# Batch 2's plain heads are turned by the DMA crossbar as its dilated heads are, its values load behind the crossing, and batch 3's dilated pairs are scored in one visit and multiplied in one

## The chip, the cores and the metric

The kernel runs on one core of a Trainium2 chip. It is one launch; the time is that of the device, in microseconds, and the number that counts is the median over several executions. One execution was taken by the hardware profiler; its times stand in the profile.

The engines that matter here: TensorE (PE; its weight loads are shown as PEld), VectorE (DVE), ScalarE (ACT), GpSimd (POOL) and SyncE (SP). Each has a queue of its own and works it off in order; they wait for each other through semaphores. DMAs are issued here by POOL (loads, which also cast f32 to bf16) and by SP (output stores, and DMA transposes through the crossbar).

## The reference

```python
def _attn_ref(q, k, v):                    # (8, 8, 576, 64) each
    B, H, S, D = q.shape
    scores = 1.0 / np.sqrt(D) * np.matmul(q, k.transpose(0, 1, 3, 2))
    rel = np.arange(S)[:, None] - np.arange(S)[None, :]
    mask_plain = (rel >= 0) & (rel < 32)
    mask_dil = (rel >= 0) & (rel < 128) & (rel % 4 == 0)
    # heads 0..3 have mask_plain, heads 4..7 mask_dil
    ...
    return np.matmul(attn, v)              # softmax over the masked scores

x = attn_out.transpose(0, 2, 1, 3).reshape(4608, 512)
h = np.maximum(x @ w_in, 0.0)              # w_in 512 x 2048
return (h * h @ w_out)                     # w_out 2048 x 512
```

## The kernel before

**Attention.** Eight batches (0 to 7) of 576 tokens and eight heads. Heads go in pairs: e = 0, 1 are the plain heads (0 to 3), e = 2, 3 the dilated ones (4 to 7). A token is 4m + r; its residue r takes the place of the dilation, so that a dilated head is four plain bands of 144 tokens. Scores come out transposed (keys on the partitions), are put through an exponential on ACT (L709), multiplied with a 0/1 mask on DVE (L711), and then multiplied with the values and with ones (numerators `o` and denominators `d`). To normalise, ACT takes the logarithm of `d` ("L", L685 and L686) and the exponential of its negative ("X", L695), and DVE multiplies (L698, and L700 for the first 16 tokens of each residue, whose sums lie apart, in `rest`: the left-over columns of other banks) into `xT`, the input of the FFN, a ring of four batches.

**Four ways to get q and k transposed.** Batches 0 and 1 are turned by TensorE. From batch 3 on, all heads are turned by DMA transposes from `qb`/`kb` into `qx`/`kx` (`cross`, L254, four per batch: k and q of tokens 0 to 255, then of the rest), and small copies put the pieces where the scores read them: "R" (`arrange`, L344 and L347: the ends of the dilated heads, eight copies), "K" and "Q" (L338, L336: the plain heads). Batch 2 (`XB`) is mixed: its dilated heads are crossed (h0 = H // 2 in `cross`), its plain heads are turned by TensorE (`trans_both`, 64 transposes at L272, copied out at L278 on DVE and L280 on ACT).

**Visits.** `quadrants(scs, pvs)` is one visit of TensorE: it scores up to two head pairs (`scs`) and multiplies up to two (`pvs`), in four 64 x 64 quadrants of the array at once (`issue`, L368). A first pair is scored into two `pa` banks (`main_s`), a second into two `pf` banks if there are products in the visit, else into `po` and `pd` (`extra`). PSUM has four `pf` banks, two `pa`, one `po` and one `pd`; the FFN's accumulators and output tiles are `pf`.

**FFN.** x @ w_in (L951), relu on ACT (L964), square on DVE (L967), then times w_out (L998), copied out by ACT or DVE (L1004) and stored by SP. The first four tiles have 256 tokens (16 groups of matmuls each), the others 512 (32 groups). Groups count on from 0: tile 3 (tokens 768 to 1023) is groups 48 to 63, the tile of tokens 1024 to 1535 begins with group 64.

**The order is written by hand.** `PROGRAM` lists, separated by "|", what is recorded after each group (the first entry before all groups): `L2:x0` is the crossing of batch 2's first part, `1s1` a step of batch 1, and so on. `steps` holds (group, rank, batch, code) for the later batches: "V032/20,21" scores pair 2 and multiplies pairs 0 and 1 of the batch before; "E20" is an exponential with its mask; "L2", "X2" a normalisation; "R00", "K00", "Q00" copies. Every engine gets its instructions in the order in which they are recorded. Around the change it stood so:

| after group | batch 2 | batch 3 |
|---|---|---|
| 32, 37 | crossing, first and second part | |
| 36 | values of the dilated heads, then the loads of batch 3's q and k, then the other values | |
| 44 | | crossing |
| 46, 47 | R copies; 64 transposes of the plain heads | |
| 48 | scores of pairs 2 and 3 (one visit) | |
| 54, 55, 59 | at 55 scores of 0 and 1 with products of 2 and 3 | R copies |
| 61 | products of 0 and 1 ... | ... with scores of 2 |
| 71 | | products of 2 with scores of 3 |
| 81 | | products of 3 with scores of 0 and 1 |
| 88 | | products of 0 and 1 |

Of the kernel before, what the change touches and what calls it, by code (L numbers as in the profile page):

```python
# [12 lines left out]
RES = 4  # L13
# [50 lines left out]
def kernel(  # L64
# [9 lines left out]
    nc = tc.nc  # L74
# [18 lines left out]
    MT = (66, M - 64)  # L93
# [157 lines left out]
    def cross(b: int, nm: str, part: int):  # L251

        n, m0, h0 = MN[part], MS[part], H // 2 if b == XB else 0
        nc.sync.dma_start_transpose(  # L254
            (qx if nm == "q" else kx)[b % 2][:, h0:, :, m0 : m0 + n].rearrange("p h c m -> p (h c) m"),
            staged(b, nm)[0:n, part, h0:, :].rearrange("p h x -> p (h x)"),
        )
# [4 lines left out]

    def trans_both(e: int):

        pools = ((ps_a, "pa"), (ps_a, "pa")) if e else ((ps_o, "po"), (ps_d, "pd"))
        for nm, copy, (pool, name) in zip("kq", (nc.scalar.copy, nc.vector.tensor_copy), pools):
            x = pool.tile([P, 1024], bf16, name=name)[:, 0:S].rearrange("p (r m) -> p r m", r=RES)
            t = staged(XB, nm)
            for r in range(RES):
                for a, m0 in enumerate(MS):  # L270
                    for hl, rows in enumerate(sides):
                        nc.tensor.transpose(  # L272
                            x[rows, r, m0 : m0 + MT[a]],
                            t[0 : MT[a], a, 2 * e + hl, D * r : D * r + D],
                            ident[0 : MT[a], 0 : MT[a]],
                        )
            if nm == "q":
                copy(qT[:, e, :, :], x)  # L278
            else:
                copy(k_flat(e).rearrange("p (m r) -> p m r", r=RES), x.rearrange("p r m -> p m r"))  # L280
# [21 lines left out]
    def load_v_rows(b: int, which="d01"):  # L302


        if "d" in which:
            vds[b] = vd_pool.tile([P, NE // 2, 2, RES * D], bf16, name="vd")
            for hl, rows in enumerate(sides):
                for e in range(NE // 2):
                    nc.gpsimd.dma_start(  # L309
                        vds[b][rows, e, :, :],  # L310
                        v[b, H // 2 + 2 * e + hl, 0:512, :].rearrange("(m p r) d -> p m (r d)", p=64, r=RES),
                    )
                for i in (0, 8):
                    nc.gpsimd.dma_start(  # L314
                        v_rows[b % 2][rows, NE // 2 :, i, :],
                        v[b, H // 2 + hl : H : 2, 64 * i : 64 * i + 64, :].rearrange("h p d -> p h d"),
                    )
# [9 lines left out]
    def arrange(b: int, what: str, g: int, jj: int, e=None, copy=nc.vector.tensor_copy):  # L327
# [42 lines left out]
    def quadrants(scs, pvs):  # L370
# [14 lines left out]
        for n, (b, e) in enumerate(pvs):  # L385
# [74 lines left out]
        for n, (b, e) in enumerate(scs):  # L460
# [6 lines left out]
            for g, c in todo:  # L467
                items = scored[n][g, c]
                if b == XB and not dil:
                    for i in range(NB) if c == g ^ crossed(b, e) else ():  # L470
                        z, y = 96 if i < 8 else 64, 96 * (i // 2)
                        out = byr(ps[i % 2][sides[c], y : y + z])
                        rows = sides[g]
                        items.append(
                            ("s", out, k_flat(e)[rows, 64 * i : 64 * i + 64], qT[rows, e, :, 16 * i : 16 * i + z // RES], z)
                        )
                    continue
# [196 lines left out]
    def natural_step(b: int, code: str):  # L674
        what, e = code[0], int(code[1])
        if what in "QKR":
            arrange(b, what, e, int(code[2]), *(int(x) for x in code[3:4]), *[nc.scalar.copy][: len(code) - 4])
# [3 lines left out]
        elif what == "L":  # L681
            _, d, rest = op[b, e]
            rec = recs[b, e] = r_pool.tile([P, 576], f32, name="rec")
            if rest[0][0] is rest[0][1]:
                nc.scalar.activation(rec[:, 0:512], d[:, :], ACT.Ln)  # L685
                nc.scalar.activation(rec[:, 512:576], rest[1][0], ACT.Ln)  # L686
# [581 lines left out]
```

## Time and profile before

| | us |
|---|---|
| runs | 297.08, 298.9, 307.21 |
| median | 298.9 |
| the profiled execution | 296.37 |
| its span (first to last instruction) | 294.6 |
| SP queue busy with DMA transposes of batch 2 (from, to) | 51.8, 57.1 |
| loads of batch 3's q and k issued on POOL | 55.7 to 59.1 |
| visits at groups 48, 55, 61, 71, 81 begin | 68.0, 74.7, 81.2, 91.1, 100.5 |

The profile gives, for each engine, the busy time, and for each instruction its line, its operands by the program's names (`xx` holds `qx` and `kx`, `pt` the exponentials, `rec` the reciprocals, `osb` output tiles), its start and length in us from the start of the span, and the idle time before it with what ended it (after "<-"). An "x3" behind a row means three instructions shown as one. The chain of waits is followed back from the last instruction, at each step to what released it. A DMA is shown where it is issued; the time to its landing is in a row of its own.

### The profile page before, as it was taken

The page shows a single profiled execution, that of the slowest core. Times are in us where ns is not written, and L with a number is a line of the kernel's source. Part 1 is how long each engine was busy: PE and PEld are TensorE (multiplying, and loading weights), DVE is VectorE, ACT ScalarE, POOL GpSimd, SP SyncE. Part 2 cuts the span into 40 slices and gives each one's busy share as a digit, 9 for nine tenths or more (in the row PEclk, how much of TensorE's full clock was granted, in tenths as well). Part 3 has the DMA queues.
Part 4 walks back from the last instruction along what each step waited for, and adds up shares of the span by engine and source line. Part 5 has one row for each costly group of instructions (what it writes and reads, how often), then busy time and mean ns, then how long its engine had stood idle before and what let it go on. Part 6 is the DMA issues. An engine that isn't in the chain of part 4 may idle for free.

```text
span 294.6 us, 8141 instructions
## 1 busy us (share of the span) xinstructions
PE 289.2 (98%) x3351; PEld 166.8 (57%) x3351; DVE 155.2 (53%) x452; ACT 187.5 (64%) x381; POOL 123.3 (42%) x208
## 2 busy tenths in 40 slices
PE   8999999999999999999999999999999999999995
PEld 7689646859555554555455545554554455445443
DVE  1786225646779656686659465947454244004400
ACT  6788636868778663988577657766776466127511
POOL 8686266756639959078563597000000000000000
PEclk9999999999999999999999999999999999999999
DMA  7999999999999999999999699012101200121022
GB/s 118 195 183 213 204 221 197 170 188 155 211 216 194 128 190 125 173 144 140 160 196 97 93 166 154 2 36 76 36 2 37 73 36 2 36 71 36 2 71 71
DMA packets 82996, 35.48 MB, mean 120 GB/s; under 512 B 52384, under 2 KB 78208, under 8 KB 82960
## 3 DMA queue, kind: packets, MB, share of 16 engines
q0 software_dynamic: 49056, 18.49, 54.8%
q1 hardware_dynamic: 33760, 16.38, 27.2%
q8 instruction: 26, 0.43, 0.6%
q10 hardware_dynamic: 144, 0.10, 0.1%
q14 instruction: 10, 0.08, 0.1%
HBM read 37.50 MB, written 9.44 MB: 159 GB/s over the span
## 4 chain that ended last, share of the span: by engine, by line
PE 96%; DMA 1%; issue 0%; POOL 0%; ACT 0%; DVE 0%; ACTq 0%; POOLq 0%
PE pf L998 43%; PE pf L951 43%; PE po L368 2%; PE pa L368 2%; DMA kb<-in_k_dram 1%; PE pf L368 1%; PE pa L773 1%; PE pd L368 1%; PE pf L825 1%; PE po L743 1%; PE pa L555 0%; PE po L863 0%; PE pd L879 0%; POOL qb L173 0%; PE pf L555 0%
## 5 line engine op out<-in xcount | busy, mean ns | idle before, releaser
L951 PE MATMUL pf<-xT,w_in 128*128 128x512 bf16 (+1 forms) x704 | 128.1, 341 | 0.0
L998 PE MATMUL pf<-w_out_sb,h2T 128*128 128x512 bf16 (+2 forms) x592 | 127.9, 373 | 0.0
L951 PEld LDWEIGHTS <-w_in 128*128 128x128 bf16 x704 | 77.9, 113 | 46.6 <-issue 0.5
L964 ACT ACTIVATE h2T<-pf 128x512 bf16<-128x512 f32 x144 | 84.2, 600 | 29.9 <-PE pf L951 29.5
L967 DVE TENSOR_TENSOR h2T<-h2T 128x512 bf16<-128x512 bf16 x144 | 60.7, 425 | 62.5 <-ACT h2T L964 59.8
L998 PEld LDWEIGHTS <-h2T 128*128 128x128 bf16 x592 | 56.1, 98 | 63.8
L1004 ACT COPY osb<-pf 128x512 f32<-128x512 f32 (+1 forms) x34 | 19.5, 575 | 52.2 <-PE pf L998 52.1
L322 POOL DMA_DIRECT2D vbd<-in_v_dram x80 | 43.5, 555 | 19.0 <-DMA kb<-in_k_dram 8.2
L173 POOL DMA_DIRECT2D qb<-in_q_dram x19 | 13.6, 721 | 12.0 <-DMA xx<-qb 10.2
L695 ACT ACTIVATE rec<-rec 128x576 f32<-128x576 f32 x24 | 16.4, 683 | 0.7
L709 ACT ACTIVATE pt<-pa 128x384 bf16<-128x384 f32 (+1 forms) x28 | 12.7, 498 | 6.3 <-DVE xT L700 3.6
L173 POOL DMA_DIRECT2D kb<-in_k_dram x19 | 13.3, 699 | 6.3 <-DMA w_in<-in_moe_w_in_dram 2.5
L195 POOL DMA_DIRECT2D vbd<-in_v_dram x16 | 10.9, 687 | 10.2 <-DMA kb<-in_k_dram 5.0
L698 DVE TENSOR_TENSOR xT<-po,rec 128x512 bf16<-128x512 f32 x14 | 9.7, 691 | 7.5 <-ACT rec L695 6.9
L314 POOL DMA_DIRECT2D vbd<-in_v_dram x20 | 12.0, 614 | 3.5 <-PE pf L951 1.6
L309 POOL DMA_DIRECT2D vd<-in_v_dram x20 | 12.2, 625 | 1.9 <-PE pf L368 1.8
L711 DVE TENSOR_TENSOR pt<-pt,mask_n 128x448 bf16<-128x448 bf16 (+1 forms) x20 | 7.1, 373 | 9.4 <-ACT pt L709 9.3
L711 DVE TENSOR_TENSOR pt<-pt,mask_f 128x384 bf16<-128x384 bf16 x24 | 8.4, 355 | 6.7 <-ACT pt L709 6.5
L698 DVE TENSOR_TENSOR xT<-pf,rec 128x512 bf16<-128x512 f32 x10 | 6.9, 691 | 8.2 <-ACT rec L695 8.2
L336 DVE COPY qT<-xx 64x576 bf16<-64x576 bf16 (+1 forms) x30 | 10.8, 358 | 0.6
L368 PEld LDWEIGHTS <-vbd 64*64 64x64 bf16 x328 | 8.1, 107 | 4.2 <-issue 3.4
L368 PE MATMUL po<-pt,vbd 64*64 64x96 bf16 (+2 forms) x196 | 8.7, 202 | 0.0
(153 smaller groups left out, 281.4 us busy)
## 6 DMA issues: line engine op xcount, KB each, us to landing
qb<-in_q_dram POOLq DMA_DIRECT2D x7, 320.0 KB, 6.9
kb<-in_k_dram POOLq DMA_DIRECT2D x7, 320.0 KB, 8.2
vd<-in_v_dram POOLq DMA_DIRECT2D x34, 64.0 KB, 4.9
w_out_sb<-in_moe_w_out_dram POOLq DMA_DIRECT2D x4, 512.0 KB, 13.7
out_dram<-osb SPq DMA_DIRECT2D x16, 128.0 KB, 4.7
qb<-in_q_dram POOLq DMA_DIRECT2D x6, 256.0 KB, 6.8
kb<-in_k_dram POOLq DMA_DIRECT2D x6, 256.0 KB, 7.7
out_dram<-osb SPq DMA_DIRECT2D x9, 160.0 KB, 3.8
```

The source lines that it names most:

```text
L173: nc.gpsimd.dma_start(t[p0 : p0 + n, part, h0:h1, :], src[b, h0:h1, t0 : t0 + RES * n, :].rearrange("h (p r) d -> p h (r d)", r=RES),)
L322: nc.gpsimd.dma_start(v_rows[b % 2][p0 + 16 * r : p0 + 16 * r + 16, e, :, :], v[b, 2 * e + hl, :, :].rearrange("(i m r) d -> r m i d", r=R ...
L368: nc.tensor.matmul(out, lhs, rhs, start=begin, stop=True, skip_group_check=True)
L695: nc.scalar.activation(rec[:, :], rec[:, :], ACT.Exp, scale=-1.0)
L698: nc.vector.tensor_tensor(out=tok[:, :, 16:M], in0=byr(o[:, :]), in1=byr(rec[:, 0:512]), op=ALU.mult)
L709: nc.scalar.activation(pt, sp[b, e][g][:, 0:n], ACT.Exp, scale=SCALE)
L711: nc.vector.tensor_tensor(out=pt, in0=pt, in1=mask, op=ALU.mult)
L951: nc.tensor.matmul(to, w_in_sb[piece][:, kt, c0 : c0 + 509 : 4], rhs, start=(kt == kts[0] and x == 0), stop=(kt == kts[-1] and x == per - ...
L964: nc.scalar.activation(hv, acc[u][:, :].rearrange("p (x n) -> p x n", x=per), ACT.Relu)
L967: nc.vector.tensor_tensor(out=hv, in0=hv, in1=hv, op=ALU.mult)
L998: nc.tensor.matmul(cur[m][:, c0:c1], h2[:, f, P * m : P * m + P], w_out_sb[:, f, c0:c1], start=(f == 0), stop=(f == NF - 1),)
L1004: (nc.vector.tensor_copy if last and part == 1 or tk0 == 3 * NT // 2 else nc.scalar.copy)(osb[:, c0:c1], cur[m][:, c0:c1])
```

## The change

- `cross` takes all eight heads of batch 2; `trans_both`, its transposes and copies, and the zeroing of padding rows for it (code "y") are gone. The plain heads of batch 2 are put in place by Q copies on DVE (groups 43 and 44) and K copies on ACT (groups 44 to 47), and scored in the way of the later batches.
- Batch 2's crossing is recorded after groups 30 and 31 instead of 32 and 37, so that its first part stands ahead of an output tile's three stores on SP. Its R copies move from group 46 to 39, ahead of batch 1's last normalisations (recorded after group 40).
- Batch 2's last values are loaded (`vwr`) ahead of batch 3's q and k instead of behind them. Code "v" now writes its placeholder tile with a small memset, and is also used once before batch 2's values.
- Batch 3: the visit at group 61 has only batch 2's products; pairs 2 and 3 are scored together at 71, and multiplied together at 79, with the scores of 0 and 1. R moves from 54, 55 and 59 to 62 and 63. The dilated heads of pair 3 of batch 3 are crossed over (`crossed`), and the loads of its values follow.
- In a visit with two scores of which the first is plain, and two products, the left-over columns lie otherwise (`rest`): numerators in both `pa` banks, denominators in the first `pf` score bank and the second `pa` bank, for both pairs. Before, each pair had one bank for both: the second `pa`, the second `pf`. "L" reads the two halves with two instructions, "X" multiplies them with two.

```diff
@@ PROGRAM (what moves) @@
-... L1:q00123 y L1:q10123 ... | 1t1dq 1cq1a | 1t1dk 1ck1 L2:x0 |  | 1s1 | 1e10 | 1e11 L2:vwd
-L3:q00123 L3:q10123 L2:vwr L2:vwp | L2:x1 1f10 | ... | L3:x f |  |  | 2t0 2t1 |  |  | v L3:Vd ...
+... L1:q00123 L1:q10123 ... | L2:x0 | 1t1dq 1cq1a L2:x1 | 1t1dk 1ck1 |  | 1s1 | 1e10 | 1e11 v
+L2:vwd L2:vwr L3:q00123 L3:q10123 L2:vwp | 1f10 | ... | L3:x f |  |  |  |  |  | v L3:Vd ...
@@ crossed @@
-        return int(1 <= b <= XB and e in (1, 3) or b >= NATURAL and e == 1 or b >= PAIRED and e == 0)
+        return int(1 <= b <= NATURAL and e in (1, 3) or b > NATURAL and e == 1 or b >= PAIRED and e == 0)
@@ cross @@
-        n, m0, h0 = MN[part], MS[part], H // 2 if b == XB else 0
+        n, m0 = MN[part], MS[part]
         nc.sync.dma_start_transpose(
-            (qx if nm == "q" else kx)[b % 2][:, h0:, :, m0 : m0 + n].rearrange("p h c m -> p (h c) m"),
-            staged(b, nm)[0:n, part, h0:, :].rearrange("p h x -> p (h x)"),
+            (qx if nm == "q" else kx)[b % 2][:, :, :, m0 : m0 + n].rearrange("p h c m -> p (h c) m"),
+            staged(b, nm)[0:n, part, :, :].rearrange("p h x -> p (h x)"),
         )
-    def trans_both(e: int):
...
@@ arrange @@
+        elif what == "K" and b == XB:
+            copy(
+                k_both[rows, g::2, hs, :].rearrange("p i h (m c j) -> p j h c i m", c=2, j=2)[:, jj, :, :, :, :],
+                kx[b % 2][src, hs, :, :].rearrange("p h c (i m) -> p h c i m", m=16)[:, :, :, g::2, :],
+            )
@@ quadrants @@
                 to = main_s[crossed(b, e)]
                 if full and scs[0][1] < NE // 2:
-                    to = (extra if n else main_s)[1]
-                rest = [to[:, 448:512]] * 2, [to[:, 384:448]] * 2
+                    rest = [t[:, 448:512] for t in main_s], [extra[0][:, 448:512], main_s[1][:, 384:448]]
+                else:
+                    rest = [to[:, 448:512]] * 2, [to[:, 384:448]] * 2
...
-                if b == XB and not dil:
-                    for i in range(NB) if c == g ^ crossed(b, e) else ():
...
@@ natural_step @@
+            elif rest[0][0] is not rest[1][0]:
+                nc.scalar.activation(rec[:, 0:512], d[:, :], ACT.Ln)
+                for g in range(2):
+                    to = sides[g ^ crossed(b, e)]
+                    nc.scalar.activation(rec[to, 512:576], rest[1][g][to, :], ACT.Ln)
...
             for g, rows in enumerate(sides) if rest[0][0] is not rest[0][1] else [(0, slice(0, P))]:
+                if rest[0][0] is not rest[1][0]:
+                    g = g ^ crossed(b, e)
@@ run @@
-        if code == "y":
-            for nm in "qk":
-                nc.gpsimd.memset(staged(2, nm)[64:80, 0, 0 : H // 2, :], 0.0)
...
-            vd_pool.tile([P, NE // 2, 2, RES * D], bf16, name="vd")
+            nc.gpsimd.memset(vd_pool.tile([P, NE // 2, 2, RES * D], bf16, name="vd")[0:32, 0, 0, 0:2], 0.0)
@@ steps @@
     for x, code in enumerate(("R00", "R01", "R10", "R11")):
-        steps.append((46, 0, XB, code))
+        steps.append((39, 0, XB, code))
+    for x, code in enumerate(("Q00", "Q01", "Q10", "Q11")):
+        steps.append((43 + x // 2, 1, XB, code))
+    for x, code in enumerate(("K00", "K01", "K10", "K11")):
+        steps.append((44 + x, 1, XB, code + "a"))
...
             if early:
-                visit(start, [(b, 2)], [(XB, 0), (XB, 1)])
+                visit(start, [], [(XB, 0), (XB, 1)])
                 for y, e in enumerate((1, 0)):
                     steps.extend([(start + y, 3, XB, f"L{e}"), (start + y + 1, 0, XB, f"X{e}")])
-            expo(2, *((start + 3, start + 6) if early else (start + 7, start + 9)))
-            visit(second, [(b, x)], [(b, 2)])
-            norm(2, second)
-            expo(x, second + 3, second + 5)
+                visit(second, [(b, 2), (b, 3)], [])
+                expo(2, second + 1, second + 2)
+                expo(3, second + 4, second + 6)
+            else:
...
         if early:
-            visit(t + 17, [(b, 0), (b, 1)], [(b, 3)])
-            expo(0, t + 18, t + 18)
-            expo(1, t + 18, t + 18)
-            norm(3, t + 18)
+            visit(t + 15, [(b, 0), (b, 1)], [(b, 2), (b, 3)])
+            steps.extend((t + 15, 3, b, f"E1{x}") for x in range(2))
+            norm(3, t + 15)
+            expo(0, t + 16, t + 16)
+            norm(2, t + 17)
...
-            steps.append(((59, 59, 54, 55)[x] if early else at + x, 1, b, code))
+            steps.append((62 + x // 2 if early else at + x, 1, b, code))
```

More of the change, by code (lines that the diff above doesn't have):

```diff
@@ L261, in k_flat @@
         return kbd[:, e, :, :].rearrange("p i c -> p (i c)")[:, 0:S]
-    def trans_both(e: int):
[L265 to L280, printed above, removed]
     def blocks(b: int, e: int, part: int):
@@ L310, in load_v_rows @@
                         vds[b][rows, e, :, :],
[L311 removed]
+                        v[b, H // 2 + 2 * e + (hl ^ crossed(b, e + NE // 2)), 0:512, :].rearrange("(m p r) d -> p m (r d)", p=64, r=RES),
                     )
+                turn_ = hl * crossed(b, 3), (1 - 2 * hl) * crossed(b, 3)
                 for i in (0, 8):
@@ L468, in quadrants @@
                 items = scored[n][g, c]
-                if b == XB and not dil:
-                    for i in range(NB) if c == g ^ crossed(b, e) else ():
[L471 to L477, printed above, removed]
                 rows, h = sides[g], 2 * e + (c ^ crossed(b, e))
@@ L676, in natural_step @@
         if what in "QKR":
-            arrange(b, what, e, int(code[2]), *(int(x) for x in code[3:4]), *[nc.scalar.copy][: len(code) - 4])
+            es = {"e": int(code[3])} if code[3:4].isdigit() else {}
+            arrange(b, what, e, int(code[2]), **es, **({"copy": nc.scalar.copy} if code[-1] == "a" else {}))
         elif what == "V":
@@ L1125, in run @@
         elif code[0] != "L":
-            batch1(code[1:]) if code[0] == "1" else trans_both(int(code[2]))
+            batch1(code[1:])
         else:
```

10 lines of the change are left out of this document (6 added, 4 removed), and 20 rows, old and new, of the table PROGRAM.

## The prediction

> **What bounds the kernel now.** I read the page first: busy time, slices, chain; then the chain of waits in order of time; then, for the stretch that the change touches (47 to 102 us), the timelines of the SP queue, POOL, DVE and ACT.
>
> ```profile
> span 294.6 us, 8141 instructions
> ...
> PE 289.2 (98%) x3351; PEld 166.8 (57%) x3351; DVE 155.2 (53%) x452; ACT 187.5 (64%) x381; POOL 123.3 (42%) x208
> ...
> PEclk9999999999999999999999999999999999999999
> DMA  7999999999999999999999699012101200121022
> ...
> PE 96%; DMA 1%; issue 0%; POOL 0%; ACT 0%; DVE 0%; ACTq 0%; POOLq 0%
> ```
>
> TensorE is the bound: 289.2 of 294.6 us, 96% of the chain, its clock full in every slice. Two things follow. A matmul taken away is worth its time; and any wait put in front of TensorE is paid in full, because there is no idle time to absorb it (5.4 us in all). The DMA engines are full through the first half, where the change puts more on them.
>
> ```profile
> 65.71 0.40 PE po L272 x16
> 66.11 0.28 PE pd L272 x16
> 66.40 0.57 PE pa L272 x32
> 66.97 1.00 PE pf L951 x8
> 67.96 0.30 PE pa L368 x20
> ...
> 68.43 6.24 PE pf L951 x56
> ...
> 75.88 5.32 PE pf L998 x24
> ...
> 82.34 1.83 PE pf L998 x8
> 84.17 6.91 PE pf L951 x32
> ```
>
> In the chain of waits (start, us, what) the rows follow each other without a hole: TensorE goes from the transposes of batch 2 (L272) to the next FFN tile, to the dilated scores of batch 2 (L368), to the visit that ends at 75.88.
>
> **The change part by part.**
>
> (a) *Transposes gone.* All 64 of L272 leave the chain: 66.97 - 65.71 = **-1.26 us**. The instruction orders differ on TensorE by these 64 matmuls alone; the scores of batch 2 and the visits of batch 3 are only put in another order, 2 scores with 2 scores, 2 products with 2 products. From nothing to a few tenths: I take **-0.2**.
>
> (b) *Crossing all heads.* The four DMA transposes of batch 2 carry eight heads instead of four, and the small copies from them (R, eight on DVE) move from group 46 to group 39, ahead of the last four normalisations of batch 1.
>
> ```profile
> 51.78 1.28 SPq L254 DMA_TRANSPOSE xx<-kb  x1
> ...
> 55.94 1.20 SPq L254 DMA_TRANSPOSE xx<-qb  x1
> ...
> 65.66 1.49 SPq L254 DMA_TRANSPOSE xx<-kb  x1
> ...
> 72.97 3.23 SPq L254 DMA_TRANSPOSE xx<-qb  x1
> ```
> ```profile
> DMA to landing us min/median/max: 4.2/6.0/7.2
> ```
> ```profile
> DMA to landing us min/median/max: 6.3/7.7/8.4
> ```
> ```profile
> 49.28 0.67 POOL L195 DMA_DIRECT2D vbd<-in_v_dram  x1 [1.33 <-DMA kb<-in_k_dram]
> ```
>
> The first fence is the SP queue, the next two the time from issue to landing of batch 2's four transfers and of batch 3's four. Batch 2, four heads: first issue 51.78, last landing 55.94 + 7.2 = 63.1, so 11.4 us. Batch 3, eight heads: 65.66 to 72.97 + 7.7 to 8.4, so about 15.3. In the changed order the first pair stands ahead of three output stores, so it can go when k has landed: POOL's row, released by that landing, says 49.28. When is the last of the eight-head transfers down? Lower end, 11.4 us again: 60.7. Upper end, the work doubled: (11.4 - 4.2) x 2 + 4.2 = 18.6, so 67.9. The nearest row is batch 3's, the same size: 49.28 + 15.3 = 64.6; the three stores now stand between the two pairs. I take **65**.
>
> [...]
>
> ```profile
> 63.04 0.49 DVE L672 TENSOR_TENSOR xT<-pa,rec 128x320 bf16<-128x320 f32 x1 [0.34 <-ACT rec L668]
> 63.45 0.17 DVE L344 COPY kbd<-xx 64x128 bf16<-64x128 bf16 x1
> ...
> 64.81 0.30 DVE L347 COPY kbd<-xx 64x128 bf16<-64x128 bf16 x1
> ```
> ```profile
> 61.26 0.42 ACT L661 ACTIVATE rec<-pf 128x320 f32<-128x320 f32 x1
> ...
> 62.92 0.57 ACT L1004 COPY osb<-pf 128x512 f32<-128x512 f32 x1
> ```
> ```profile
> 50.17 0.70 ACT L560 COPY xx<-pa 128x640 bf16<-128x640 bf16 x1
> ```
>
> What is queued behind: R's first copy reads the last transfer, so DVE stands until 65. Behind it are eight copies (63.45 to 65.11: 1.66 us) and then the four L672. ACT's third L661 writes a buffer that the first L672 (0.49) has to free, so ACT stands too. From there, 61.26 to 62.92 (1.66 us) to the output copy L1004; after it the changed ACT order has three of the four new K copies (no such row; the nearest, 128x640 in 0.70, is twice as many partitions and from PSUM, DVE's 64-row copies are shorter: 0.6 each), then the second L1004. That frees the fourth `pf` bank for the next tile at landing + 1.66 + 0.49 + 1.66 + 0.57 + 1.8 + 0.57 = landing + 6.75. TensorE wants it after eight matmuls, the dilated scores and four more matmuls (0.111 each, 6.24 / 56): 68.43 + 0.45 = 68.9, less 1.26: 67.6. So the point from which it decides is a landing at 60.9, and every us after it costs one. At 65: **+4.1**; ends 0 and +7.0. In the kernel before, R came behind the L672, so a late landing held nobody. The other new copies (Q on DVE, the fourth K) replace those of L278 and L280 and lie beside FFN matmuls: nothing.
>
> (c) *Denominator ends in the score banks.* In a visit with two scores and two products the ends of rows now lie in both `pa` banks, and their denominators in the first `pf` score bank.
>
> ```profile
> 75.27 1.15 ACT L709 ACTIVATE pt<-pf 128x448 bf16<-128x448 f32 x2
> 76.31 0.59 ACT L685 ACTIVATE rec<-pf 128x512 f32<-128x512 f32 x1
> ...
> 77.64 0.91 ACT L709 ACTIVATE pt<-pa 128x448 bf16<-128x448 f32 x2
> ```
> ```profile
> 78.64 0.22 DVE L700 TENSOR_TENSOR xT<-pf,rec 128x64 bf16<-128x64 f32 x1
> ...
> 79.90 0.69 DVE L698 TENSOR_TENSOR xT<-po,rec 128x512 bf16<-128x512 f32 x1
> ```
> ```profile
> ACT pt L709 <- DVE xT L700: 3.6, 4, 0.9
> ```
>
> Before, the first exponential starts at 75.27, 0.6 us before the visit ends, and hands its bank to the matmul at 75.88. Now that bank takes denominators until the visit's last matmuls, so neither exponential starts before 75.9, and the next output tile gets the bank of the second: +1.15, the whole row. The same form occurs in the new visit of batch 3 at group 79: twice, **+2.3** (0.5 to 1.4 each).
>
> Then the exponentials at 77.64 read a bank that the L700 of the head before now reads too. That ACT waits for such a DVE read is in the waits (3.6 us in 4 cases); L700 ends at 78.86, so 1.2 later. Behind it on ACT are L685 and L695 of the next head, behind those the L698 that ended at 80.59, 0.6 before the next visit (81.20). With 0.6 + 1.2 more on ACT and 1.15 more on TensorE that leaves about nothing: **+0.3** (0 to 0.5).
>
> [...]
>
> (d) *Batch 3's R copies to groups 62 and 63*, ahead of an output copy on DVE.
>
> ```profile
> 82.11 0.60 ACT L685 ACTIVATE rec<-pf 128x512 f32<-128x512 f32 x1 [2.25 <-PE pf L368]
> ```
> ```profile
> 83.58 0.69 DVE L698 TENSOR_TENSOR xT<-pf,rec 128x512 bf16<-128x512 f32 x1 [1.51 <-ACT rec L695]
> ...
> 84.31 0.68 DVE L1004 COPY osb<-pf 128x512 f32<-128x512 f32 x1
> ```
>
> The copy frees the fourth bank of the next tile. It ends 2.9 us after the L685 that follows the visit; with four copies (0.83) ahead, 3.7, and 0.15 from the visit to L685: 3.9. TensorE wants the bank 1.83 (row 82.34) + 6 x 0.216 (6.91 / 32) = 3.1 after the visit: **+0.7** (0 to 1). The loads of batch 3's q and k are issued four small loads later on POOL; before, its first crossing waited for an output store on SP, not for them, so that costs nothing unless (b) is worse than taken. The two memsets that go and the two that come are on POOL, with nobody waiting.
>
> Sum: -1.26 - 0.2 + 4.1 + 2.3 + 0.3 + 0.7 = **+5.9 us**. The profiled execution took 296.4 us (span 294.6 and 1.8 around it), 2.5 below the median, 298.9; on the median that gives 304.8, and I say **305**. About 2% (6.0 us) is what a measurement of this kernel can tell from no change, so the forecast stands on the edge, just over it.
>
> **The rivals.**
>
> [...] Chance 0.2.
>
> *Only the gain*: the waits of (c) and (d) are hidden too, for instance if the bank handed to the next tile is an earlier one. -1.5, **297.4**. Against: TensorE's wait for the second exponential stands in the changed order. Chance 0.05.
>
> *The backlog goes on*: the transfers land at 67.9, so (b) is +7.0, batch 3's crossing, which waits on SP for the output copy that (b) holds up, lands later still, and its R copies stand on DVE at group 62 in front of the bank of (d). With the upper ends of (c) and (d): -1.3 + 7.0 + 2.8 + 0.5 + 1.0 = +10, **308.9**. It decides from a landing at about 67. [...] Chance 0.2.
>
> *Faster by over 2%*: 6 us would have to come out of 1.5 us of removed work and 5.4 of idle time. 0.03.
>
> **How the numbers follow.** The forecast has the rest, 0.52, and its own range of 302.5 to 307 (landing 63 to 67); three fifths of that lie over the bound, 304.9. Slower: 0.6 x 0.52 + 0.2 = 0.52. Faster 0.03. Within: 0.45. For 8 in 10 the range leaves out the gain and the far end of the backlog: 299.5 to 309.
>
> **What would show it.** (a) No L272. (b) A gap on DVE from about 59 us, ended by the DMA of the q crossing, longest among DVE's waits, ACT idle beside it, and a hole of TensorE at 66 to 70. If that copy starts before 61, (b) is wrong. (c) A hole of about 1.1 us after each visit at groups 55 and 79, ended by an exponential; without it, (c) is wrong. (d) A hole of some 0.7 after the first matmuls of the tile at group 64. A row of TensorE's clock under 9 in a slice would speak for the backlog.

## The result and the profile after

| | before | after |
|---|---|---|
| median of six executions, us | 297.7 (296.91 to 307.21) | 310.4 (309.67 to 312.24) |
| span of the profiled execution, us | 294.6 | 309.4 |
| mean granted clock of TensorE over that span (1 is full) | 1.000 | 0.983 |

The changed kernel is slower: ratio 1.044, 95% interval 1.041 to 1.048. The forecast was 305.0, from 299.5 to 309.0: the right side, 5.4 us short, and outside the range. (A ratio leaves out executions more than 1.5% above the fastest of the same kernel; where a kernel's executions spread widely it lies below the ratio of the medians.)

The page of the changed kernel, the rows that answer to those of before:

```profile
span 309.4 us, 8023 instructions
...
PE 294.5 (95%) x3287; PEld 168.3 (54%) x3287; DVE 159.1 (51%) x456; ACT 192.1 (62%) x383; POOL 121.2 (39%) x208
...
PEclk9999999996799999999999999999999999999999
...
PE 67%; DMA 24%; ACT 2%; DVE 2%; issue 2%; POOL 2%; SPq 0%; ACTq 0%; POOLq 0%
```

Two things are new. DMA has 24% of the chain of waits, which was almost TensorE's alone (96%); and TensorE is busy 5.3 us longer with 64 matmuls fewer, because its clock was under full in two slices, the tenth and eleventh (70 to 85 us). What TensorE waited for (us in total, times, longest):

```profile
PE pf L937 <- ACT osb L990: 3.2, 1, 3.2
PE pf L937 <- ACT rec L639: 2.3, 2, 2.1
PE pf L984 <- ACT pt L695: 2.0, 2, 1.0
PE po L729 <- DVE kbd L1008: 1.1, 1, 1.1
PE pa L354 <- DMA vbd<-in_v_dram: 0.8, 1, 0.8
PE pf L937 <- DVE osb L990: 0.7, 1, 0.7
PE po L354 <- DVE xT L682: 0.6, 1, 0.6
PE pf L937 <- DVE xT L882: 0.6, 1, 0.6
```

Only the fourth (L729, start-up) was there before; the last lies at 16 us, in the start as well. The first two belong to step (b), the third and the seventh to (c), the sixth to (d); the fifth, late values of batch 1, to none. (Lines of the changed kernel: L937 and L984 are the two FFN products, L990 the output copy, L354 the visits, L330 and L333 the R copies, L319 the K copies, L639 to L650 batch 1's normalisations, L695 the exponentials, L682 and L686 the multiplications of batches 2 and later, L253 the crossing.) The stretch in which most of the time went, in the chain of waits (start, us, what):

```profile
58.54 8.52 DMA xx<-qb
...
67.08 0.19 DVE kbd L330
...
69.07 0.53 DVE kbd L333
69.60 0.03 issue
69.63 0.50 DVE xT L650
...
71.83 0.57 ACT osb L990
72.40 1.52 ACT kbd L319
73.92 1.59 ACT kbd L319
75.53 1.31 ACT kbd L319
76.83 0.03 issue
76.86 0.59 ACT osb L990
77.45 0.04 issue
77.50 2.73 PE pf L937 x12
```

Here it can be read off in order what stood behind what: the last transfer of the crossing (down at 67.06), eight R copies until 69.60, a normalisation and the logarithms, an output copy, three K copies of 1.3 to 1.6 us, and the second output copy, whose bank TensorE had wanted for 3.2 us. The same stretch by windows (length, busy time and count of PE, PEld, DVE, ACT, POOL, granted clock, DMA share, GB/s):

```profile
66.00:70.00 4.00, 2.59 (x12) 1.09 (x11) 2.85 (x9) 0.00 (x0) 4.00 (x6) 1.00 1.37 153
70.00:74.00 4.00, 3.13 (x52) 2.17 (x52) 3.01 (x8) 3.77 (x7) 2.13 (x5) 0.71 1.61 184
74.00:78.00 4.00, 0.83 (x5) 0.44 (x4) 0.21 (x1) 3.94 (x4) 3.19 (x6) 0.50 1.75 183
78.00:82.00 4.00, 4.00 (x21) 2.74 (x20) 2.29 (x7) 3.94 (x9) 3.14 (x5) 0.51 1.41 192
82.00:94.00 12.00, 10.33 (x161) 7.06 (x159) 6.70 (x20) 7.88 (x17) 4.93 (x10) 1.00 1.44 181
```

The clock was full while TensorE stood at 68.6 to 70.6, half soon after, and full again from 82 on. A matmul at half clock looks like work, so the 3.7 us lost in this way show up nowhere among the waits.

Where the 14.8 us between the two profiled executions went, from the starts of the same pieces of work on TensorE's timeline:

| up to | later than before by, us | of which new | what |
|---|---|---|---|
| middle of batch 1's work (54.95, before 53.10) | 1.85 | 1.85 | the execution's start; the kernels are the same up to the loads; run 1, with the same start, was 0.2 ahead of before |
| output tile at 62.37 | 2.87 | 1.02 | late values of batch 1 (0.80 hole) |
| first tile after it, 70.64 | 3.74 | 0.87 | transposes gone -1.26, hole 2.06 |
| visit at group 55, 85.41 | 10.81 | 7.07 | holes 0.23 and 3.17, the rest (3.67) half clock |
| first matmul behind it, 87.74 | 11.88 | 1.07 | hole 1.02 |
| visit at 61, 93.73 | 12.60 | 0.72 | hole 0.65 |
| visit at 71, 104.70 | 13.69 | 1.09 | hole 0.72 in the tile of group 64 |
| products behind the visit at 79, counted behind the next visit, 123.36 | 14.94 | 1.25 | hole 1.02 |

Without the start it is 13.1, beside 12.7 between the medians.

### The profile page after: what moved, and what is told of

Same layout as the page of the kernel before. It is cut to its first block, busy times and chain, and to the rows that moved or that the text cites. A ratio compares the mean times of both kernels' runs of the same rounds, so it can differ in the third digit from the quotient of the medians.

```text
span 309.4 us, 8023 instructions
## 1 busy us (share of the span) xinstructions
PE 294.5 (95%) x3287; PEld 168.3 (54%) x3287; DVE 159.1 (51%) x456; ACT 192.1 (62%) x383; POOL 121.2 (39%) x208
## 4 chain that ended last, share of the span: by engine, by line
PE 67%; DMA 24%; ACT 2%; DVE 2%; issue 2%; POOL 2%; SPq 0%; ACTq 0%; POOLq 0%
PE pf L937 32%; PE pf L984 32%; DMA xx<-qb 7%; DMA qb<-in_q_dram 6%; DMA w_in<-in_moe_w_in_dram 3%; DMA w_out_sb<-in_moe_w_out_dram 3%; DMA vbd<-in_v_dram 2%; DMA kb<-in_k_dram 2%; ACT kbd L319 1%; PE po L354 1%; PE pf L354 1%; PE pa L354 1%; DVE kbd L333 1%; DMA out_dram<-osb 1%; POOL qb L172 1%
## 5 line engine op out<-in xcount | busy, mean ns | idle before, releaser
L937 PE MATMUL pf<-xT,w_in 128*128 128x512 bf16 (+1 forms) x704 | 131.5, 346 | 6.9 <-ACT osb L990 3.2
L984 PE MATMUL pf<-w_out_sb,h2T 128*128 128x512 bf16 (+2 forms) x592 | 127.8, 374 | 2.0 <-ACT pt L695 2.0
L937 PEld LDWEIGHTS <-w_in 128*128 128x128 bf16 x704 | 79.0, 115 | 56.1 <-issue 8.8
L953 DVE TENSOR_TENSOR h2T<-h2T 128x512 bf16<-128x512 bf16 x144 | 60.9, 425 | 63.2 <-ACT h2T L950 60.5
L984 PEld LDWEIGHTS <-h2T 128*128 128x128 bf16 x592 | 56.2, 98 | 65.8 <-issue 2.0
L990 ACT COPY osb<-pf 128x512 f32<-128x512 f32 (+1 forms) x34 | 19.5, 574 | 50.2 <-PE pf L984 50.0
L695 ACT ACTIVATE pt<-pa 128x384 bf16<-128x384 f32 (+1 forms) x26 | 11.7, 498 | 5.0 <-DVE xT L686 4.9
L194 POOL DMA_DIRECT2D vbd<-in_v_dram x16 | 10.9, 693 | 6.7 <-DMA kb<-in_k_dram 2.6
L682 DVE TENSOR_TENSOR xT<-po,rec 128x512 bf16<-128x512 f32 x13 | 9.0, 692 | 7.7 <-ACT rec L679 7.4
L682 DVE TENSOR_TENSOR xT<-pf,rec 128x512 bf16<-128x512 f32 x11 | 7.6, 692 | 10.3 <-ACT rec L679 10.3
L317 DVE COPY qT<-xx 64x576 bf16<-64x576 bf16 (+1 forms) x34 | 12.2, 360 | 0.6
L354 PEld LDWEIGHTS <-vbd 64*64 64x64 bf16 x328 | 8.8, 107 | 5.9 <-issue 4.4
L695 ACT ACTIVATE pt<-pf 128x448 bf16<-128x448 f32 (+1 forms) x18 | 8.3, 519 | 1.6 <-PE pf L354 1.0
```

What stands on the lines that cost most here:

```text
L354: nc.tensor.matmul(out, lhs, rhs, start=begin, stop=True, skip_group_check=True)
L682: nc.vector.tensor_tensor(out=tok[:, :, 16:M], in0=byr(o[:, :]), in1=byr(rec[:, 0:512]), op=ALU.mult)
L695: nc.scalar.activation(pt, sp[b, e][g][:, 0:n], ACT.Exp, scale=SCALE)
L937: nc.tensor.matmul(to, w_in_sb[piece][:, kt, c0 : c0 + 509 : 4], rhs, start=(kt == kts[0] and x == 0), stop=(kt == kts[-1] and x == per - ...
L953: nc.vector.tensor_tensor(out=hv, in0=hv, in1=hv, op=ALU.mult)
L984: nc.tensor.matmul(cur[m][:, c0:c1], h2[:, f, P * m : P * m + P], w_out_sb[:, f, c0:c1], start=(f == 0), stop=(f == NF - 1),)
```

## The experiments

Each kernel was run beside the kernel before; ratios are to that. Times are medians. Runs 1, 2, 3 and 5, and 8, have the changed kernel's line numbers; in the others the same lines are up to some 30 away.

**1. R behind the normalisations.** Theory 1 is that the order on DVE and the K copies on ACT make the holes, and the holes the half clock. Its rival is that the landing itself is what TensorE waits for.

```diff
-        steps.append((39, 0, XB, code))    # R00 R01 R10 R11
+        steps.append((40, 0, XB, code))
```

> Against the changed kernel only the order on DVE differs: batch 2's eight R copies stand behind batch 1's last four normalisations (group 40) instead of ahead of them (group 39). Theory 1 (the wait at the head of DVE's queue, then the slow K copies on ACT, make the holes at 68 to 78 us, and the holes bring the halved clock of 72 to 81 us): the 2.06 us hole ended by the logarithm L639 goes; the normalisations are over by about 66; the scores wait some 0.2 us for R (landing 67.06 + 2.55 = 69.6, TensorE there at about 69.5); the second output copy still stands behind three K copies of 1.5 us and ends at about 71.6, wanted at 70.6, so a hole of about 1 instead of 3.17. Holes 5.5 -> 1.3, and with no long hole the clock stays full, another 3.7: 310.4 - 7.9 = 302.5, range 300.5 to 305. Rival (it is the landing itself, TensorE needs what R writes in any order): the hole moves to the scores, the time stays within 1.5 us of 310.4.

Measured 301.58 us (four executions, 300.87 to 303.77), ratio 1.012 (1.006 to 1.018): 8.8 us less than the changed kernel, for one order of eight copies. DVE's timeline:

```profile
63.10 0.49 DVE L650 TENSOR_TENSOR xT<-pa,rec 128x320 bf16<-128x320 f32 x1 [0.34 <-ACT rec L646]
67.65 0.44 DVE L330 COPY kbd<-xx 64x128 bf16<-64x128 bf16 x1 [4.05 <-DMA xx<-qb]
67.76 0.48 DVE L333 COPY kbd<-xx 64x128 bf16<-64x128 bf16 x1
68.25 0.57 DVE L330 COPY kbd<-xx 64x128 bf16<-64x128 bf16 x1
68.36 0.61 DVE L333 COPY kbd<-xx 64x128 bf16<-64x128 bf16 x1
69.00 0.19 DVE L330 COPY kbd<-xx 64x128 bf16<-64x128 bf16 x1
```

DVE still stands 4 us for the same transfer, landed at 67.62, but with the normalisations behind it in time and not in the queue, nobody else stands with it. What TensorE now waits for lies at the scores of group 48, holes of 1.03, 0.97 and 0.65 us:

```profile
PE pa L354 <- DVE kbd L333: 1.6, 2, 1.0
PE pa L354 <- issue: 1.0, 1, 1.0
```

The first (1.03) has no releaser in the trace, but it ends at 67.71, just behind the landing, and the scores there read the transfer's own tile (`xx`); the other two wait for R. So the rival has a part of 1 us; for the rest theory 1 holds. The clock is not wholly saved: two of the four executions had a mean clock of 0.994 and took 302.2 and 303.8, the two with 1.000 took 300.9 and 301.0. The same program costs some 2 us more where the clock falls. How much of that is the clock and how much longer holes can't be told, since only one of the four has a trace.

**2. K copies on DVE.**

```diff
-        steps.append((44 + x, 1, XB, code + "a"))    # K00 K01 K10 K11
+        steps.append((44 + x, 1, XB, code))
```

> Against the changed kernel only this differs: batch 2's four K copies are made by DVE instead of ACT, after the same groups. Theory 1: the two output copies then follow each other on ACT, the second ends at about 73.0 instead of 77.45, before TensorE wants its bank (74.3): the hole of 3.17 us goes, the one of 2.06 before it stays. The clock still falls at 71.7, since that follows the first hole, but comes back earlier (it came back 4.4 us after TensorE went on): about 1.6 of the 3.7 us is saved. 310.4 - 3.2 - 1.6 = 305.6, range 303.5 to 307. Rival (the copies are as slow on DVE, 1.5 us each, and hold up the squares): no more than 1 us is gained. Rival (the second hole alone brings the clock down): the clock stays full, 303.5.

Measured 308.41 us, but from 304.17 to 311.94 in four executions; ratio 1.028 (1.017 to 1.038). The median is outside the expected 303.5 to 307. The 3.17 us hole is gone as theory 1 has it, and K on DVE took 0.88 each (3.51 for four), not 1.5. But the profiled execution, the slowest, had a new hole of 4.6 us at the tile of group 64, and DVE shows why:

```profile
91.57 0.21 DVE L686 TENSOR_TENSOR xT<-pa,rec 128x64 bf16<-128x64 f32 x1
95.73 0.19 DVE L330 COPY kbd<-xx 64x128 bf16<-64x128 bf16 x1 [3.94 <-DMA xx<-qb]
95.84 0.29 DVE L333 COPY kbd<-xx 64x128 bf16<-64x128 bf16 x1
96.14 0.19 DVE L330 COPY kbd<-xx 64x128 bf16<-64x128 bf16 x1
96.25 0.30 DVE L333 COPY kbd<-xx 64x128 bf16<-64x128 bf16 x1
96.39 0.68 DVE L990 COPY osb<-pf 128x512 f32<-128x512 f32 x1
```

Batch 3's last transfer landed at 95.7, and its R copies stand ahead of the output copy L990: the same trap as batch 2's, one batch later. That it shuts in some executions and not in others, by the landing of each, would explain the spread; only one has a trace. So this run alone could not price K; run 8 below does.

**3. Both.**

> Both edits: R behind the normalisations, K copies on DVE. Theory 1: nothing but the 0.2 to 0.3 us wait of the scores for R is left of the 5.5 us of holes, and the clock stays full: 310.4 - 5.2 - 3.7 = 301.5, range 300 to 303. What is left over the kernel before (297.7) is then the visits at groups 55, 61 and 79 and the tile at 64 (1.1 + 0.7 + 1.2 + 1.2), 1.0 for the late values of batch 1, less 1.26 for the transposes. Rival (the landing itself): within 1.5 us of 310.4.

Measured 301.60 us (300.69 to 305.69), ratio 1.012 (1.006 to 1.018), as expected, and no better than run 1: once R is out of the way, three K copies on ACT are over before TensorE wants the bank (in run 1 they lie at 64.90 to 69.46, and no wait for the second output copy is left). The profiled execution, the slowest at 305.69, again had the hole of the second trap (2.6 us, with half clock behind it).

**4. The second bank's exponential first** (at groups 55 and 79; the tile `pt` is now taken by whichever of the two comes first, which is not shown in the cut).

```diff
-    steps += [(55, 3, XB, "E10"), (55, 3, XB, "E11"), ...
+    steps += [(55, 3, XB, "E11"), (55, 3, XB, "E10"), ...
...
-            steps.extend((t + 15, 3, b, f"E1{x}") for x in range(2))
+            steps.extend((t + 15, 3, b, f"E1{x}") for x in (1, 0))
```

> Against the changed kernel only this differs: after the visits at groups 55 and 79 the exponential of the second score bank is made ahead of that of the first (ACT and DVE order alone). The second bank has no denominators of the rows' ends in it, so its exponential needn't wait for the visit's last matmuls, and the next output tile takes that bank. Theory (step c of the prediction: the hole of 1.02 us after each of the two visits is the wait for two exponentials in a row): each hole shrinks by 0.5 to 1.0, 310.4 - 1.5 = 308.9, range 308.2 to 309.5. Rival (the next output tile would then wait for the other bank, or something else is late): no change, 310.1 to 310.7.

Measured 309.77 us (308.76 to 310.70), 0.6 less than the changed kernel, inside the spread; the time doesn't decide. The trace does: the wait of L984 for L695 (2.0 us, twice 1.0) is gone from TensorE's list, and the second bank's exponential starts before the visit is over:

```profile
85.48 0.48 ACT L696 ACTIVATE pt<-pf 128x384 bf16<-128x384 f32 x1
86.24 0.54 ACT L696 ACTIVATE pt<-pf 128x448 bf16<-128x448 f32 x1 [0.27 <-PE pf L354]
```

Only the first bank's, with the denominators in it, still waits for the visit's matmuls (L354; L696 are the exponentials here). Ahead of the visit at 61 the hole grows from 0.65 to 1.3: TensorE is there earlier, ACT isn't.

**5. Run 1 and batch 3's R later** (groups 64 and 65 for 62 and 63).

> R of batch 2 behind batch 1's normalisations, as in the first run, and batch 3's R copies two groups later (64 and 65 instead of 62 and 63), behind the output copy of the tile before. Theory (step d of the prediction: R stands ahead of that copy on DVE, and where batch 3's crossing lands late the copy stands for it too): the hole of 0.66 us at the tile of group 64 goes, and so do the long ones (2.6 and 4.6 us with a halved clock behind them) that single executions of the two kernels with K on DVE had: 301.58 - 0.7 = 300.9, range 300.2 to 301.4, and a narrow spread. Rival (R's results are wanted just as early): the scores at group 71 wait instead, 301.5 or more.

Measured 301.36 us (300.17 to 302.86), ratio 1.013 (1.005 to 1.021). The 0.7 us hole at group 64 is gone from the trace, but the median is only 0.2 below run 1: too little to tell.

**6. R in the order of the landings, and both exponentials swapped.**

```diff
-    for x, code in enumerate(("R00", "R01", "R10", "R11")):
+    for x, code in enumerate(("R10", "R11", "R00", "R01")):
         steps.append((40, 0, XB, code))
```

> The kernel with both R moves, and two more orders changed: of batch 2's R copies the four that read the first tokens' transfers (landed at about 59.5) come first, so that only four, 1.1 us, are left after the last landing (67.6) instead of eight, 2.2; and the second score bank's exponential goes first at groups 55 and 79. Theory: the scores of group 48 start 1.1 us earlier, the holes of 2.65 us there shrink to about 1.5 and the clock, which fell for 3.3 us, stays full: -1.1 - 1.7; the two holes behind the visits go (-2.0) and 0.65 of it comes back ahead of the visit at 61, whose exponentials wait as before: -1.35. 300.9 - 4.1 = 296.8, range 296 to 299, so no slower than the kernel before (297.9). Rival (the clock falls again, since about 1.5 us of holes remain): 298.5. Rival (the landing, not the copies behind it, sets the scores): 299.5.

Measured 299.09 us (ten executions, 298.54 to 300.75), ratio 1.0067 (1.0035 to 1.0099). The clock stays full in the profiled execution (one of the ten has a mean of 0.993), four copies are made at 63 to 64, four after the landing, and of the 2.65 us of holes at the scores 1.4 are left. It is just outside the expected 296 to 299 and near the second rival's 299.5: the gain is smaller than forecast, because the transfer itself (67.1) now sets the scores.

**7. The crossing's second pair ahead of the stores, K on DVE.**

```diff
-... | L2:x0 | 1t1dq 1cq1a L2:x1 | 1t1dk 1ck1 | ...
+... | L2:x0 L2:x1 | 1t1dq 1cq1a | 1t1dk 1ck1 | ...
```

> As the run before, with batch 2's K copies on DVE, and with the crossing's second pair recorded right behind its first, ahead of the output tile's three stores on SP. Theory (the stores cost the second pair some 1.5 us in the queue): the last landing moves from 67.6 to about 66, the scores of group 48 wait for nothing, 296.8 - 1.0 = 295.8, range 295 to 297. Rival (the three stores now go some 5 us later, there are three output buffers, so the output copies at about 63 wait for them and the FFN's next banks with them): slower than the run before by 1 to 3 us. Rival (the transfers are limited by what the DMA engines carry): the landing stays at 67, no change.

Measured 299.06 us (ten executions, 297.16 to 303.58), ratio 1.0046 (1.0005 to 1.0086). The last landing is at 65.7 in place of 67.1, and TensorE's list has nothing of batch 2's crossing any more (the first row is the visit at 61; L720 and L928 are start-up, L975 four short gaps):

```profile
PE po L344 <- DVE xT L672: 1.3, 1, 1.3
PE po L720 <- DVE kbd L999: 1.1, 1, 1.1
PE pf L975 <- issue: 0.6, 4, 0.2
PE pf L928 <- DVE xT L873: 0.5, 1, 0.5
```

So in this order a landing by 66 is early enough; the prediction's 60.9 was for the order with R, the normalisations and the K copies behind the landing. In this trace TensorE waits for nothing that the late stores hold. The expected 295.8 was still missed by 3 us, and the executions spread over 6. The profiled one, 298.76, was 1.5 us late before batch 1's scores were over (54.58, before 53.10); what the slower ones lose, no trace shows. The run has two edits, and what each gave is not separated.

**8. K on DVE, batch 3's R later.** It prices K without the second trap.

> The kernel with K on DVE alone (R of batch 2 still ahead of the normalisations; 304 to 312 in single executions), and batch 3's R copies two groups later. Theory 1: the spread came from batch 3's crossing landing late (95.7) with its R copies ahead of an output copy on DVE; with R behind it, the second hole and its fall of the clock (4.6 + some 2.5 us in the profiled execution) can't happen, and what is left over the kernel with both moves is the hole at the head of DVE's queue (2 to 4 us at 66 to 70) and the half clock behind it (some 2.5 us): 304.5, range 303 to 306, narrow. The K copies then account for some 5 us of the changed kernel's time, the order of R for the rest. Rival (K on DVE was of no use, the 308 is what it is worth): 307 to 309.

Measured 304.48 us (304.13 to 305.62), ratio 1.024 (1.020 to 1.028): as expected, and narrow. That the spread is gone with batch 3's R behind the copy fits the second trap of run 2. What is left over run 1 is the hole at the head of DVE's queue (3.2 us in this trace, ended by L639) and the half clock behind it. With that, the changed kernel's K copies on ACT account for 5.9 us of its 310.4 (with the 0.7 of batch 3's R in it), the order of R for 8.8; the two overlap, since either edit alone keeps the second output copy from its long wait.

**9. Batch 3's part alone, on the kernel before.**

> The kernel before with only the batch 3 part of the change: pairs 2 and 3 scored together at 71 and multiplied together at 79 with the new places for the rows' ends, R at 62 and 63; batch 2 as before, its plain heads transposed by TensorE, its dilated heads alone crossed. Theory (steps c and d add up by themselves): one hole of 1.0 us after the visit at 79 and 0.7 to 1.2 at the tile of group 64, 297.9 + 1.9 = 299.8, range 299 to 300.6. Rival (these waits come only with the late crossing of batch 2): within 0.5 us of 297.9.

Measured 298.80 us (ten executions, 297.68 to 300.10), ratio 1.0043 (1.0011 to 1.0076), 1.6 over the kernel before in the same runs (297.17), where 1.9 was expected. Its waits are those of steps (c) and (d), each once (L721 are the exponentials there, L1016 the output copy, L963 and L1010 the FFN):

```profile
PE pf L1010 <- ACT pt L721: 1.0, 1, 1.0
PE pf L963 <- DVE osb L1016: 0.7, 1, 0.7
```

They add to 1.7. These costs don't come from the late crossing.

**10. All four exponentials of batch 2's plain heads ahead of the normalisations**, on top of run 7.

```diff
-    ... (55, 3, XB, "E10"), (55, 3, XB, "L3"), (56, 0, XB, "X3")]
-    steps += [(56, 1, XB, "E00"), (56, 1, XB, "E01"), (57, 3, XB, "L2"), ...
+    ... (55, 3, XB, "E10"), (55, 3, XB, "E00"), (55, 3, XB, "E01")]
+    steps += [(55, 3, XB, "L3"), (56, 0, XB, "X3"), (57, 3, XB, "L2"), ...
```

> As the kernel with the second pair ahead of the stores (299.06), and at group 55 all four exponentials of batch 2's plain heads stand ahead of the two normalisations. Theory: what is left there is the 1.3 us hole ahead of the visit at 61, which waits for the po bank that the second normalisation frees; ACT loses 1.14 us of that chain waiting for DVE's reading of the pa bank (L676) before the third exponential, and with the new order it doesn't: the hole shrinks to 0.2 to 0.5. 299.06 - 0.9 = 298.2, range 297.3 to 298.7; the medians of single executions with a late crossing stay. Rival (the first normalisation, now 0.9 us later on ACT, gives back a bank that the output tiles want): no gain, 299 or more.

Measured 297.23 us (twelve executions, 296.69 to 298.52), ratio 0.9996 (0.9973 to 1.0019): the change with these orders put right, and K on DVE, can't be told from the kernel before. The hole ahead of the visit at 61 is 0.4, as expected; the gain on run 7's median, 1.8, is twice the expected one, but the intervals of the two ratios overlap. In its profiled execution batch 3's crossing (down at 88.9) makes DVE late, and the products at 79 wait 1.3 us for masks: about what the missing transposes had saved.

**11. Batch 3's loads ahead of batch 2's last values**, on top of run 10.

> As the kernel with all four exponentials ahead (297.23, no different from the kernel before), and the loads of batch 3's q and k stand ahead of batch 2's last values on POOL again, as in the kernel before. Theory (the four loads that the change put in front make batch 3's crossing later: its last landing at 88.9 holds DVE for 4 us, and the products at 79 wait 1.3 us for DVE's masks): the landing comes 1 to 3 us earlier, the 1.3 us go: 296.2, range 295.5 to 297.0. Rival (batch 2's values then come late for the visits at 55 and 61): 298 or more. Rival (the DMA engines are full, the order of the loads changes only which of them lands first): the same as 297.2.

A miss of the expected 295.5 to 297.0: 298.85 us (twelve executions, 296.46 to 301.18), ratio 1.0027 (0.9993 to 1.0062). Batch 3's last landing came earlier, 83.2 in place of 88.9, but batch 2's came later, 68.0 in place of 64.0, and the scores of group 48 waited 1.9 us. Nothing waits for batch 2's values at the visits at 55 and 61, so the first rival has the time but not the cause. The second fits the landings, though it expected the time to stay at 297.2: in this stretch the order of the loads would only decide which transfer lands first. It isn't shown: there is one profiled execution of each, and runs 7 and 10, with the same order up to there, already differ by 1.7 us in batch 2's landing (65.7 and 64.0).

## Why the prediction was right in sign and short in size

**What failed is step (b): the landing and the K copies were too short in its sum, and the half clock that its hole sets off was not in it.** It put the freeing of the fourth `pf` bank at "landing + 6.75". The trace has 77.45 - 67.06 = 10.4. The terms:

| term | forecast, us | measured, us |
|---|---|---|
| last landing | 65 | 67.06 |
| TensorE's late start in this execution | none | -1.85 |
| R copies | 1.66 | 2.55 |
| normalisation to first output copy | 2.72 | 2.80 |
| three K copies on ACT | 1.8 | 4.4 |
| second output copy | 0.57 | 0.59 |
| half clock behind the bank | none | 2.2 |

The K copies were priced at 0.6 from two rows that were both unlike them: an ACT copy from PSUM and DVE copies of another layout. They were 1.5. Up to the visit at 55 the table of where the time went has 1.02 + 0.87 + 7.07 us, and with the 1.26 that the missing transposes gave back 10.2 us of losses, against +4.1. Of the difference, 3.6 are the longer way to the bank (0.9 of R, 2.6 of K), 0.2 the landing as TensorE saw it, and 2.2 the half clock of the 52 matmuls behind it (7.98 us on the timeline in place of 5.8 at 0.111).

**The landing looks right only by luck.** The first pair was issued at 48.09, 1.2 us ahead of the 49.28 that the step took, and the four transfers took 19.0 us instead of 15.7; that the 2.1 us cost so little is due to an execution in which TensorE was itself 1.85 late. In runs 1 to 6 and 8 the landing is at 66.9 to 67.6, with TensorE on time in all but run 3 (0.4 late). Run 4 has the changed kernel's order up to the visit at 55 and TensorE on time (53.09, before 53.10):

```profile
PE pf L938 <- ACT rec L639: 4.0, 1, 4.0
PE pf L938 <- ACT osb L991: 3.2, 1, 3.2
```

There the landing, 66.92, costs 1.9 us more than forecast, R takes 1.7 as forecast, the K copies again cost 2.6 too much, and the half clock behind the bank 2.7 (8.45 in place of 5.8): the visit at 55 begins at 84.88, before at 74.60, which with the 1.26 is 11.5 us for step (b).

What was lost ahead of the bank, the 0.8 us for late values of batch 1 and the first 1.5 us of half clock, cost nothing by itself: TensorE would have stood for the bank that much longer. The late values were not foreseen (the last of their loads was issued at 53.83 and landed at 61.77, before 52.66 and 56.63; that the crossing, which now goes ahead of them, is the reason is likely but not shown). Runs 1 and 8 show the mechanism as the prediction put it: R at the head of DVE's queue holds ACT and through it TensorE.

**The half clock was in no term of the forecast.** The prediction has a clock under 9 only as a sign of the backlog, and in no slice of the kernel before is it under 9. That was the wrong condition: a kernel without holes cannot show what holes do to the clock. In these traces the clock falls behind holes, whatever makes them (3.2 us ended by ACT's logarithm in run 8, 4.6 ended by DVE's output copy in run 2), and the step's own +4.1 was already longer than the 2.06 us behind which it fell here. Nor is the clock of the kernel before always full: of its 66 executions beside these runs, six had a mean clock of 0.994 and took 299.6 to 301.7 us, the others 296.0 to 299.7. Where it fell in the six, no trace shows.

**(a)** No L272 in the trace: -1.26, right. The further -0.2 for reordered visits can't be seen in it.

**(c)** Holes of 1.02 behind each of the two visits (1.15 forecast) and 0.65 ahead of the visit at 61 (0.3): with what lies beside them 3.0 for 2.6. Runs 4 and 9 show both the cause and the size.

**(d)** The hole of 0.72 was where it was put, at 0.7; the stretch lost 1.1. Runs 5 and 9 agree with it.

**The rivals.** A landing by 61, the lower end of step (b) (60.7, chance 0.2), did not come: the 1.18 MB (q and k, 8 heads x 576 x 64 in bf16) took 19.0 us from first issue (48.09) to last landing (67.06), with POOL's loads issued in between, and each of the four transfers took 8.5 to 10.4 us to land. The backlog rival gave 308.9, nearest to the result, and was more nearly right than its chance of 0.2: by its own words it decides from a landing at about 67, and 67.06 was measured. But its +7.0 for (b) is the landing alone, at 67.9; the 10.2 measured have the K copies and the half clock in them. Its second half was real: batch 3's crossing was issued from 73.7 (before: 65.7), behind the stores of the output copies that were held up, its last transfer landed at 93.7 (before: 81.0), and in run 2 its R copies did stand in front of the bank of (d). One step of the chances is off as well: of a range of 302.5 to 307 a little under half lies over 304.9, not three fifths, which takes "slower" from 0.52 to about 0.44 and touches no term of the sum.

## What to carry to other kernels

Before a copy that waits for a DMA is moved up in an engine's order, list what stands behind it on that engine and on the engines that wait for those; here one group's difference for eight small copies was 8.8 us. Price a new copy from a row of the same engine, source and layout, or give it a range that reaches to the slowest row, and multiply by the number of copies that stand in one queue. Where TensorE never waits, ask of every new hole not only its length but what clock the work behind it gets: here, at a granted clock of 0.50, twelve matmuls behind the bank took 2.73 us, 0.228 each in place of 0.111.

## What the runs showed of the hardware

*How fast the clock falls.* The windows of run 2, whose hole has no work in it (columns as above):

```profile
65.68:68.50 2.82, 0.00 (x0) 0.00 (x0) 1.53 (x8) 0.00 (x0) 1.51 (x4) 0.95 1.46 195
68.50:69.63 1.13, 0.00 (x0) 0.00 (x0) 0.98 (x3) 0.45 (x2) 0.35 (x1) 0.50 1.46 195
69.63:75.00 5.37, 5.37 (x61) 3.65 (x61) 4.48 (x8) 3.46 (x8) 3.90 (x7) 0.50 1.52 158
75.00:75.50 0.50, 0.50 (x7) 0.46 (x5) 0.49 (x2) 0.45 (x1) 0.50 (x2) 0.95 1.61 126
```

TensorE stops at 65.68; a mean of 0.95 over 2.82 us means that the clock halved about 2.5 us later; work goes on at 69.63 and the clock is back at about 75.0, 5.4 us later. So this hole of 4 us cost an estimated 2.7 us more, half of the 5.4. In other traces the clock fell 2.2 us (run 8), 2.5 (run 4), 3.0 (run 2's second hole) and 3.1 (the changed kernel, with a few matmuls in between) after TensorE had stopped. In run 1's profiled execution, one of the two in which it fell, no hole was longer than 1.03 us; three, of 2.65 us together, lay within 3.3 us. Single holes of 1.02 us behind the visits of the changed kernel, and one of 1.3 ahead of run 7's visit at 61, left it at 1.00. What decides whether a hole brings the clock down, and why it fell in some executions of one program and not in others, is not shown.

*Small DVE copies beside POOL's loads.* In the traces of the changed kernel and of runs 1 and 5 the R copies took 0.19 and 0.30 us, or 0.44 to 0.61; the long ones lie beside the same four loads that POOL issues (L194, 2.96 us together), as in run 1, where the copies after 69.0 are short again; in run 2, where these loads were over by 66.45, all eight, from 66.93 on, took 0.19 to 0.30. That the loads are the cause is not shown: in run 6 four R copies (63.27 to 64.14) took 0.19 to 0.33 us, with POOL busy for 0.88 us of 63.0 to 64.0.

*K copies.* 64 x 640 and 64 x 512 elements in bf16, both sides in SBUF, strided: 1.60 and 1.31 us on ACT in the changed kernel, 0.88 on average on DVE in run 2 (3.51 for four); batch 3's, of another layout, 0.3 to 0.6 on DVE (0.65 for two in the kernel before, 1.11 for two in the changed one). Why the same copies take ACT so much longer than DVE is open, as is whether matmuls put into the holes would have held the clock; that wasn't tried.
